# Rows of score maxima written by VectorE, an earlier place for the first expert slot's tokens, and two DMAs for the norm's gains

## The chip, the cores and the metric

One NeuronCore of one Trainium2 chip runs the whole program. The metric is the device time of one execution in microseconds (us), and smaller is better. The engines are named as in the profile: PE (matrix multiplications and transposes), DVE (VectorE), ACT (ScalarE), POOL (GpSimd) and SP (which issues most DMAs).

## The reference

Attention with normalized queries and keys feeds a mixture of experts in which each token goes to one expert:

```python
def _attn_ref(q, k, v, g_q, g_k):          # q, k, v: (8, 12, 448, 64)
    def rmsnorm(x, g):
        return x / np.sqrt(np.mean(x * x, axis=-1, keepdims=True) + 1e-06) * g
    q_n, k_n = (rmsnorm(q, g_q), rmsnorm(k, g_k))
    scores = np.matmul(q_n, k_n.transpose(0, 1, 3, 2)) / np.sqrt(64)
    scores = scores - np.max(scores, axis=-1, keepdims=True)
    attn = np.exp(scores)
    attn = attn / (np.sum(attn, axis=-1, keepdims=True) + 1e-09)
    return np.matmul(attn, v)

def _moe_ref(x, modality_id, w_gate, modality_bias, w1, w2):   # x: (3584, 768), 8 experts, F = 1024
    logits = x @ w_gate + modality_bias[modality_id]
    e_idx = np.argmax(logits, axis=1)
    probs = softmax(logits)
    for e in range(8):
        mask = e_idx == e
        h = np.maximum(x[mask] @ w1[e], 0.0)
        out[mask] = probs[mask, e][:, None] * (h @ w2[e])
```

All arrays are float32. The kernel keeps that precision by splitting operands into a rounded high part and a rest, and summing the products of parts.

## The kernel before, in words

**Attention** runs over 48 units; a unit is two heads of one batch entry. One loop walks steps n from -22 to 335, seven steps to a unit; each step j of unit u issues one block of 128 score rows. For each unit, `load` brings q and k, `sumsq` (line 836) squares them on ACT and sums the squares on DVE, `rstd` and `norm` (line 886) scale them, `tr` (line 900) transposes them on PE and splits them into parts, with the product of the two gain vectors, `gs`, multiplied into k. The four DMAs of `load_gains` (line 127) fetch the gains, `gain_product` (line 133) multiplies them.

Scores are computed twice. First `sa` (line 979) makes the high parts' product in blocks of 128 rows, and DVE takes each block's negated maxima into a column of `mx` (128 x 7; `at_hlw` in the rows). `mt` (line 998) transposes `mx` on PE to 7 x 128; ACT copies that from PSUM to `ms`, and a DMA lays the seven rows end to end as one row, number 64 of the tile `ql`. It is issued from ACT's queue for units 0, 1 and 45 to 47, else from SP's. Then `st` (line 1011) makes the scores transposed, with full parts: a matmul with 128 rows, and a second with 65, in which row 64 of the keys' tile `kh` is all ones, so that the row of maxima is subtracted. ACT takes the exponential, `av` (lines 1051 to 1060) multiplies with the values, and `avcopy` (line 1067) copies the result out of PSUM, on ACT for most units. `sa` and `tr` have two PSUM buffers each, `st` two, `av` one. In the first units PE also runs filler matmuls (`warm`, line 1341), whose number at each step is in the table `PLAN`.

**The experts** run on 14 static slots of 256 tokens and a tail. Of the first slot the tokens are brought in while attention ends: `xgather` (line 550) gathers them on POOL's queue, `xkeep` (line 555) stores them to DRAM, `xfetch` (line 559) fetches them back in four pieces, both on SP's queue, and `xturn` (line 574) transposes a third of them on DVE; ACT then casts the third to its high part in `xw`, and DVE takes the rest. `split1` (line 531) splits the first weights in the same way. The first expert matmul is `ph` (line 608).

**The order of the work** is written out, not found by the hardware: `PLAN` (line 34) gives the step at which each piece is due, and the loop (lines 1424 to 1544) hands pieces to lists that are emptied at a step: `pre["A"]` on ACT and `pre["V"]` on DVE ahead of the step's exponential, `post` behind it. Each engine executes its own list strictly in that order and waits on semaphores.

In the rows, `w1w`, `xw`, `r2w`, `xrw`, `at_hlw` and similar are large tiles that several buffers share; line L52 is a helper through which DVE, ACT and POOL instructions are recorded. `w1w` holds `ql`, and `w1w<-xw 7x128` is thus the row of maxima.

## Time and profile before

| | us |
|---|---|
| median of three runs | 1041.73 |
| lowest and highest | 1040.16, 1044.53 |
| profiled execution | 1043.32 |
| its span in the trace | 1041.5 |
| PE busy | 1017.7 (98%) |
| DVE, ACT, POOL busy | 742.2 (71%), 710.0 (68%), 718.2 (69%) |

The profile is one execution; what lies outside the span (1.8 us) is start and end. Attention takes the first 541 us or so, the experts the rest. [...]

### The profile page before, as it was taken

To read this page: it belongs to the slowest core of one execution; us is meant where nothing else is said; L and a number is where in the kernel's file an instruction comes from. 1 tells how busy PE (TensorE), PEld (TensorE's weight loads), DVE (VectorE), ACT (ScalarE), POOL (GpSimd) and SP (SyncE) were. 2 spreads that over 40 slices of the span, in tenths; PEclk is the share of its full clock that TensorE was granted. 3 is DMA by queue.
4 is the path that set the end of the run, shared out by engine and by line. 5 is a ranking of instruction groups with operands and counts; after the bars stand their busy time and mean duration, and the time that the engine had idled before them with its cause. 6 is when DMAs were issued, how large, how long until landed. Compare 5 with 4: busy or idle time off the path is not lost.

```text
span 1041.5 us, 18863 instructions
## 1 busy us (share of the span) xinstructions
PE 1017.7 (98%) x6462; PEld 820.2 (79%) x6462; DVE 742.2 (71%) x1260; ACT 710.0 (68%) x1379; POOL 718.2 (69%) x747
## 2 busy tenths in 40 slices
PE   8999999999999999999999999999999999999996
PEld 7655666666666666656659999999999999999995
DVE  5777888887888778886667987755675567656740
ACT  6897999889999889887655555645554455545531
POOL 6788798989788887888956646765645555565451
PEclk9999999999999999999999999999999999999998
DMA  6775658868677677665748506234572343234261
GB/s 181 193 172 131 160 139 191 166 143 183 157 170 160 156 177 156 163 119 119 230 120 285 92 17 188 71 92 122 162 263 74 110 122 92 62 92 123 74 201 63
DMA packets 147960, 148.20 MB, mean 142 GB/s; under 512 B 72762, under 2 KB 137742, under 8 KB 147344
## 3 DMA queue, kind: packets, MB, share of 16 engines
q1 hardware_dynamic: 122458, 105.08, 42.7%
q0 software_dynamic: 25328, 41.82, 12.8%
q8 instruction: 53, 0.87, 0.4%
q14 instruction: 51, 0.42, 0.2%
q10 hardware_dynamic: 70, 0.02, 0.0%
HBM read 150.31 MB, written 33.39 MB: 176 GB/s over the span
## 4 chain that ended last, share of the span: by engine, by line
PE 85%; DMA 4%; DVE 3%; ACT 3%; issue 2%; POOL 1%; SPq 1%; ACTq 0%; POOLq 0%; DVEq 0%
PE ph L608 23%; PE py L638 22%; PE st L1018 12%; PE av L1060 10%; PE sa L990 5%; PE av L1056 3%; PE tr L908 3%; PE xt L1126 2%; PE sm L1082 2%; DVE at_hlw L52 1%; PE sm L1089 1%; DMA w1w<-xw 1%; PE mt L1001 1%; DMA xrw<-xg 1%; DMA r<-in_q_dram 1%
## 5 line engine op out<-in xcount | busy, mean ns | idle before, releaser
L608 PE MATMUL ph<-xw,w1w 128*128 128x256 f32 x2016 | 246.3, 283 | 2.1 <-ACT at_w2lw L52 1.3
L608 PEld LDWEIGHTS ph<-xw,w1w 128*128 128x128 f32 x2016 | 243.9, 192 | 3.9 <-ACT at_w2lw L52 1.4
L52 DVE TENSOR_REDUCE at_hlw<-sa 128x1 f32<-128x448 f32 x336 | 205.0, 619 | 30.3 <-PE sa L985 15.2
L1018 PE MATMUL st<-w1w 128*128 128x448 f32 (+1 forms) x480 | 183.4, 431 | 1.5 <-ACT r2w L52 0.9
L52 POOL DMA_INDIRECT r<-in_moe_w_dram,tb_w x60 | 84.6, 1411 | 54.9 <-DVE w1w L52 39.7
L52 ACT ACTIVATE hhw<-ph 128x512 fp32r<-128x512 f32 x56 | 33.5, 598 | 123.4 <-PE ph L608 94.3
L52 ACT ACTIVATE r2w<-st 128x448 f32<-128x448 f32 x168 | 91.1, 545 | 34.6 <-PE st L1018 23.2
L638 PE MATMUL py<-w2lw,hhw 128*128 128x384 f32 x448 | 113.7, 334 | 0.0
L52 DVE TENSOR_TENSOR w1w<-r,w1w 128x768 fp32r<-128x768 f32 x112 | 104.9, 968 | 11.0 <-ACT w1w L52 9.8
L990 PE MATMUL sa<-w1w 128*128 128x448 f32 (+1 forms) x288 | 108.1, 376 | 3.0 <-DVE at_hlw L52 1.2
L52 ACT CAST w1w<-xw 64x448 fp32r<-64x448 f32 x188 | 105.9, 563 | 3.7 <-issue 1.4
L52 POOL DMA_INDIRECT r2w<-in_moe_w_dram,tb_vi x48 | 51.5, 1074 | 81.7 <-DVE w2lw L52 68.1
L52 DVE TENSOR_TENSOR w2lw<-r2w,w2ha 128x1536 fp32r<-128x1536 f32 x28 | 49.1, 1757 | 80.0 <-ACT w2ha L52 49.2
L1018 PEld LDWEIGHTS st<-w1w 128*128 128x128 f32 (+1 forms) x480 | 86.0, 190 | 24.6 <-issue 10.9
L1018 PE MATMUL st<-w1w,w2ha 65*128 65x448 f32 x288 | 100.6, 370 | 0.5 <-DMA w1w<-xw 0.5
L52 ACT ACTIVATE at_w2lw<-st 128x448 f32<-128x448 f32 x168 | 90.6, 545 | 12.5 <-PE st L1018 5.7
L52 POOL TENSOR_TENSOR xrw<-r,at_hlw 112x512 f32<-112x512 f32 x95 | 97.8, 1050 | 0.5
L52 POOL TENSOR_TENSOR r2w<-r2w 128x448 f32<-128x448 f32 (+1 forms) x72 | 83.3, 1157 | 21.3 <-DVE r2w L52 15.0
L52 ACT CAST w1w<-r 128x768 fp32r<-128x768 f32 x112 | 95.2, 903 | 0.1
L52 ACT ACTIVATE yw<-py,ltn 128x384 f32<-128x384 f32 x55 | 29.4, 579 | 77.0 <-PE py L638 48.5
L638 PEld LDWEIGHTS py<-w2lw,hhw 128*128 128x128 f32 x448 | 80.9, 188 | 0.0
L52 POOL TENSOR_TENSOR r2w<-r2w,at_w2lw 64x448 f32<-64x448 f32 (+1 forms) x48 | 55.3, 1151 | 32.8 <-DVE r2w L52 17.4
(302 smaller groups left out, 2210.2 us busy)
## 6 DMA issues: line engine op xcount, KB each, us to landing
w1w<-xw SPq DMA_DIRECT2D x216, 112.0 KB
xg<-xrw SPq DMA_DIRECT2D x14, 768.0 KB
xrw<-xg SPq DMA_DIRECT2D x56, 192.0 KB
r<-in_q_dram SPq DMA_DIRECT2D x19, 448.0 KB
r<-in_k_dram SPq DMA_DIRECT2D x19, 448.0 KB
w2ha<-xw SPq DMA_DIRECT2D x72, 112.0 KB
w1w<-w1w SPq DMA_DIRECT2D x48, 112.0 KB
r2w<-in_v_dram SPq DMA_DIRECT2D x24, 224.0 KB
```

Of the source, the lines that this page charges most:

```text
L52: return fn(*a, **kw)
L608: PE.matmul(ps[:, i], lhsT=lt_, rhs=rt_[:, c], start=n == 0, stop=n == 17)
L638: PE.matmul(ps[n][:, :384], lhsT=lt_[:, j, 128 * t : 128 * t + 128], rhs=rt_[:, 384 * n : 384 * n + 384], start=j == 0 and m == 0, stop=j ...
L908: PE.transpose(sp[:, c], src[:, c], idn[:CP, :CP])
L990: PE.matmul(ps[:, :S], lhsT=t["qq"][r, h, a : a + 128], rhs=t["kk"][h][r], start=True, stop=True)
L1001: PE.transpose(ps[0:NJ, :128], t["mx"], idn)
L1018: PE.matmul(ps[:, :S], lhsT=l, rhs=t["qq"][:, h] if first else t["ql"][0:65, h], start=first and (j != 3 or h == 0), stop=not first and (j ...
L1056: PE.matmul(t["av"][:, :S], lhsT=vd_b[u % 2], rhs=t["p"][:, 3], start=False, stop=True)
L1060: PE.matmul(t["av"][64 * h : 64 * h + 64, :S], lhsT=vv[:, u % 3, j], rhs=t["p"][:, j], start=c == 0, stop=False)
L1082: PE.matmul(R[g][32 * i : 32 * i + 32, :S], lhsT=sel[:, m], rhs=T[u + i // 2]["cs"][:, i % 2], start=m == 0, stop=False, tile_position=(0, ...
L1089: PE.matmul(sm[32 * i : 32 * i + 32, :S], lhsT=wg[:, (4 * g + i) % NP], rhs=T[4 * g + i]["xt"], start=False, stop=True, tile_position=(0, ...
L1126: PE.transpose(ps[:CP, 128 * c : 128 * c + 128], T[u]["xt"][:, c * CP : (c + 1) * CP], idn)
```

## The change

**Rows of maxima.** For units 0, 1, 45, 46 and 47 (`by_rows`) `mx` is the last seven columns of a tile of 71 whose first 64 are zero. `mt` transposes all 71, so that the maxima land on partitions 64 to 70 of PSUM. One DVE multiplication of 7 x 896 then writes rows 64 to 70 of `ql`: the seven rows, repeated seven times along the row, times a block of the identity, so that row 64 + j holds the maxima of block j at their place and zeros elsewhere. The keys' tiles get seven rows of ones, and the second score matmul of these units has 71 rows. ACT's copy and the DMA of these units go.

**Gains.** `load_gains` issues two DMAs, each of which reads a gain vector twice and writes 128 partitions. `gain_product` is called ahead of the norm of queries of unit 0 instead of behind the norm of its keys.

**First slot.** `xkeep` moves from step 317 to 315, `xfetch` from 320 to 317, and the three `xturn` from steps 330, 332, 334 to 327, 329, 331. `split1` in unit 47 moves from its steps 1 and 4 to 4 and 6.

**Fillers.** The `warm` entries of steps -7, -6 and -5 go (three, one and one).

```diff
-'warm': {-22: 15, -21: 3, -20: 1, -16: 4, -15: 1, -13: 5, -10: 2, -7: 3, -6: 1, -5: 1, 5: 1, 7: 1}
+'warm': {-22: 15, -21: 3, -20: 1, -16: 4, -15: 1, -13: 5, -10: 2, 5: 1, 7: 1}
...
-'s1': (1, 4)
+'s1': ((1, 4), (4, 6))
...
-            for half in range(2):
-                SY.dma_start(gg[64 * half : 64 * half + 64, 0:1], g_q.unsqueeze(1))
-                SY.dma_start(gg[64 * half : 64 * half + 64, 1:2], g_k.unsqueeze(1))
+            for i, g in enumerate((g_q, g_k)):
+                SY.dma_start(gg[:, i : i + 1], bass.AP(tensor=g.tensor, offset=g.offset, ap=[[0, 2], [1, 64], [1, 1]]))
...
+    KR = 64 + NJ
+    kh_f = [view(w2ha, WZ * i, KR, WZ) for i in range(3)] + [view(w1w, 4 * ST, KR, WZ)]
...
+    mw_b = [view(sw, SS + 288 + 72 * i, 128, KR) for i in range(2)]
+    mx_b = [m[:, 64:KR] for m in mw_b]
+
+    def by_rows(u):
+        return u < 2 or u >= NU - 3
...
+            G.memset(kh[64:KR].bitcast(F32), 1.0)
...
+        for m in mw_b:
+            G.memset(m[:, 0:64], 0.0)
...
+            if by_rows(u):
+                PE.transpose(ps[0:KR, :128], mw_b[u % 2], idn)
+                sh = [NJ, NJ, 128]
+
+                def rows():
+                    V.tensor_tensor(
+                        out=t["ql"][64:KR].rearrange("p h s -> p (h s)").rearrange("p (j c) -> p j c", j=NJ),
+                        in0=ps[64:KR, :128].unsqueeze(1).to_broadcast(sh),
+                        in1=idn[64:KR, 64:KR].unsqueeze(2).to_broadcast(sh), op=ALU.mult)
+
+                return rows
...
+                    kr = 128 if first else KR if by_rows(u) else 65
+                    PE.matmul(ps[:, :S], lhsT=l[:kr], rhs=t["qq" if first else "ql"][:kr, h],
...
-        LD0, XRJ = 0, (1, 3, 5)
+        LD0, XRN = 0, (327, 329, 331)
...
-                at(pre["A"], n + 1, mt(*a))
+                at(pre["V" if by_rows(*a) else "A"], n + 1, mt(*a))
...
+                if a == (0, 0):
+                    gain_product()
                 norm(*a, V if a in P["nv"] else G)
-                if a == (0, 1):
-                    gain_product()
...
-            if n == NJ * (NU - 3) + 2:
+            if n == 315:
                 xkeep(0)
-            if n == NJ * (NU - 3) + 5:
+            if n == 317:
                 xfetch(0)
-            if i >= NU - 2 and j in P["s1"]:
-                split1(P["s1"].index(j), i - NU + 2)
+            if i >= NU - 2 and j in P["s1"][i - NU + 2]:
+                split1(P["s1"][i - NU + 2].index(j), i - NU + 2)
```

Three pieces of the engines' lists show how instructions move. On DVE, in the first norms (`at_hlw<-xrw` is a sum of squares, `xrw<-r_0` the norm of unit 0's queries), before:

```order
L52 TENSOR_REDUCE at_hlw<-xrw 112x8 x2
L52 TENSOR_TENSOR gs<-gg 128x1
L52 TENSOR_SCALAR gs<-gs 128x1
L52 TENSOR_REDUCE at_hlw<-xrw 112x8 x2
L52 MEMSET w2ha 65x3x64
L52 MEMSET w1w 65x64
L52 TENSOR_TENSOR xrw<-r_0_158,at_hlw 112x2x4x64
```

The same place after the change:

```order
L52 TENSOR_REDUCE at_hlw<-xrw 112x8 x4
L52 TENSOR_TENSOR gs<-gg 128x1
L52 TENSOR_SCALAR gs<-gs 128x1
L52 MEMSET w2ha 71x3x64
L52 MEMSET w1w 71x64
L52 TENSOR_TENSOR xrw<-r_0_158,at_hlw 112x2x4x64
```

The gains' product stands behind four sums of squares instead of between two and two.

On DVE around the maxima of unit 0 (`at_hlw<-sa` are maxima of unit 1, `mt` the transposed maxima of unit 0), before:

```order
L52 TENSOR_REDUCE at_hlw<-xrw 112x8
L52 SCALAR_TENSOR_TENSOR xw<-tr_1_386,gs,xw 128x448
L52 TENSOR_REDUCE at_hlw<-sa_0_423 128x1
L52 TENSOR_REDUCE at_hlw<-sa_1_430 128x1
L52 TENSOR_REDUCE at_hlw<-sa_2_434 128x1
```

The same place after the change:

```order
L52 TENSOR_REDUCE at_hlw<-xrw 112x8
L52 SCALAR_TENSOR_TENSOR xw<-tr_1_386,gs,xw 128x448
L52 TENSOR_TENSOR w1w<-mt_391,idn 7x896
L52 TENSOR_REDUCE at_hlw<-sa_0_417 128x1
L52 TENSOR_REDUCE at_hlw<-sa_1_424 128x1
L52 TENSOR_REDUCE at_hlw<-sa_2_428 128x1
```

A multiplication of 7 x 896 stands ahead of the maxima of unit 1.

On ACT at the passage from attention to the experts (`xw<-r2w` casts a third of the tokens, `xrw<-av45` copies the result of unit 45, `st47` are exponentials of unit 47, `w1w<-r1_1` is a weight split), before:

```order
L52 ACTIVATE r2w_163<-st46_5_6296 128x448
L52 ACTIVATE r2w_163<-st46_6_6306 128x448
L52 COPY xrw_160<-av45_6241 128x448
L52 ACTIVATE lo6_6248<-lo6_6248 112x32
L52 ACTIVATE at_w2lw_167<-st47_0_6314 128x448
L52 ACTIVATE at_w2lw_167<-st47_1_6325 128x448
L52 CAST w1w_161<-r1_1_159 128x768
L52 ACTIVATE at_w2lw_167<-st47_2_6337 128x448
L52 CAST xw_162<-r2w_163 128x512
```

The same place after the change:

```order
L52 ACTIVATE r2w_163<-st46_5_6286 128x448
L52 ACTIVATE r2w_163<-st46_6_6297 128x448
L52 CAST xw_162<-r2w_163 128x512
L52 COPY xrw_160<-av45_6232 128x448
L52 ACTIVATE lo6_6239<-lo6_6239 112x32
L52 ACTIVATE at_w2lw_167<-st47_0_6307 128x448
L52 ACTIVATE at_w2lw_167<-st47_1_6319 128x448
L52 CAST xw_162<-r2w_163 128x512
L52 ACTIVATE at_w2lw_167<-st47_2_6330 128x448
```

The cast of the first third stands ahead of the copy of av45, where it stood behind three exponentials of unit 47 and a weight split; that split stands later. On SP no row changes its place.

## Rows read from the trace of the kernel before

**Rows 1.** The page, part 1: busy us, share of span, instructions.
```profile
PE 1017.7 (98%) x6462; PEld 820.2 (79%) x6462; DVE 742.2 (71%) x1260; ACT 710.0 (68%) x1379; POOL 718.2 (69%) x747
```

**Rows 2.** Busy time by stretches: PE, PEld, DVE, ACT, POOL, granted clock, DMA, GB/s.
```profile
core 0: us, PE busy (x) PEld busy (x) DVE busy (x) ACT busy (x) POOL busy (x), PEclk, DMA share, GB/s
11.90:15.30 3.40, 3.27 (x16) 3.28 (x16) 1.35 (x3) 3.34 (x9) 2.36 (x7) 0.51 0.48 147
100.00:490.00 390.00, 387.66 (x2124) 243.76 (x2124) 319.69 (x637) 345.46 (x802) 328.40 (x369) 1.00 0.71 157
528.00:538.00 10.00, 8.56 (x44) 4.96 (x43) 7.67 (x10) 7.33 (x17) 6.06 (x6) 1.00 0.31 88
```

**Rows 3.** Timeline, all engines, 5 to 13 us: start, us, engine, line, operation.
```profile
6.97 0.32 SPq L833 DMA_DIRECT2D r<-in_q_dram  x1
7.55 1.15 ACT L52 ACTIVATE xrw<-r 112x512 f32<-112x512 f32 x2 [0.83 <-DMA r<-in_k_dram]
...
9.10 0.60 PE L908 MATMUL tr<-idn,xrw 112*128 112x112 f32 x4 [0.27 <-POOL xrw L52]
...
9.61 0.16 DVE L52 TENSOR_TENSOR gs<-gg 128x1 f32<-128x1 f32 x1 [3.57 <-DMA gg<-in_g_k_dram]
...
9.88 1.27 DVE L52 TENSOR_REDUCE at_hlw<-xrw 112x8 f32<-112x512 f32 x2
11.35 0.62 DVE L52 TENSOR_TENSOR xrw<-r,at_hlw 112x512 f32<-112x512 f32 x1
...
12.03 1.01 PE L908 MATMUL tr<-idn,xrw 112*128 112x112 f32 x4 [2.08 <-DVE xrw L52]
```

**Rows 4.** Timeline, PE, ACT and DVE around the maxima of unit 0.
```profile
25.20 1.73 PE L1341 MATMUL warm<-idn,ones 128*128 128x128 f32 x14
26.05 0.24 ACT L52 CAST xw<-mt 7x128 fp32r<-7x128 f32 x1
...
26.32 1.32 ACTq L52 DMA_DIRECT2D w1w<-xw  x1
...
27.17 1.81 DVE L52 TENSOR_REDUCE at_hlw<-sa 128x1 f32<-128x448 f32 x3 [0.31 <-PE sa L990]
...
27.68 0.56 ACT L52 CAST w1w<-xw 64x448 fp32r<-64x448 f32 x1 [1.39 <-issue]
...
30.48 0.44 PE L1018 MATMUL st<-w1w,w2ha 65*128 65x448 f32 x1 [0.49 <-DMA w1w<-xw]
```

**Rows 5.** The page, part 5: two groups of 128x768, mean ns of one.
```profile
L52 DVE TENSOR_TENSOR w1w<-r,w1w 128x768 fp32r<-128x768 f32 x112 | 104.9, 968 | 11.0 <-ACT w1w L52 9.8
...
L52 ACT CAST w1w<-r 128x768 fp32r<-128x768 f32 x112 | 95.2, 903 | 0.1
```

**Rows 6.** Waits of SP's queue, 495 to 545 us: in total, times, longest.
```profile
SPq L556 <- DMA xrw<-x_d,ltn: 7.4, 1, 7.4
...
SPq L562 <- DMA xg<-xrw: 5.0, 1, 5.0
```

**Rows 7.** Timeline, PE, ACT and DVE at the passage to the experts.
```profile
527.71 0.53 ACT L52 COPY xrw<-av 128x448 f32<-128x448 f32 x1 [0.15 <-PE av L1056]
...
528.42 1.72 PE L1060 MATMUL av<-r2w,at_w2lw 128*64 128x448 f32 x8
...
530.65 1.19 DVE L52 STREAM_TRANSPOSE r2w<-xrw 128x512 f32<-128x512 f32 x1 [1.82 <-DMA xrw<-xg]
...
531.88 0.62 ACT L52 CAST xw<-r2w 128x512 fp32r<-128x512 f32 x1 [0.47 <-DVE r2w L52]
...
537.56 1.70 PE L608 MATMUL ph<-xw,w1w 128*128 128x256 f32 x12 [1.25 <-ACT at_w2lw L52]
...
539.81 0.38 PE L608 MATMUL ph<-xw,w1w 128*128 128x256 f32 x1 [0.54 <-ACT xw L52]
...
540.53 0.85 PE L608 MATMUL ph<-xw,w1w 128*128 128x256 f32 x5 [0.35 <-DVE xw L52]
...
541.32 0.97 PE L1060 MATMUL av<-at_w2lw 128*64 128x448 f32 x4
```

**Rows 8.** The page, part 3: main DMA queue, packets, MB, share of 16 engines.
```profile
q1 hardware_dynamic: 122458, 105.08, 42.7%
```

More of the change, by code (lines that the diff above doesn't have):

```diff
@@ L453 @@
     kk_f = [view(w1w, ST * i + W, 128, WZ) for i in range(4)]
-    kh_f = [view(w2ha, WZ * i, 65, WZ) for i in range(3)] + [view(w1w, 4 * ST, 65, WZ)]
+    KR = 64 + NJ
+    kh_f = [view(w2ha, WZ * i, KR, WZ) for i in range(3)] + [view(w1w, 4 * ST, KR, WZ)]
     zeros = [view(t, o, p, n, d)[:, :, S : S + 64] for t, o, p, n, d in (
-        (w1w, W, 128, 4, ST), (w2ha, 0, 65, 3, WZ), (w1w, 4 * ST, 65, 1, WZ))]
+        (w1w, W, 128, 4, ST), (w2ha, 0, KR, 3, WZ), (w1w, 4 * ST, KR, 1, WZ))]
     def two(t):
@@ L484 @@
     ra_b, rz_b = SS + 48 * 4, SS + 48 * 5
-    mx_b = [view(sw, SS + 288 + 8 * i, 128, NJ) for i in range(2)]
+    mw_b = [view(sw, SS + 288 + 72 * i, 128, KR) for i in range(2)]
+    mx_b = [m[:, 64:KR] for m in mw_b]
+    def by_rows(u):
+        return u < 2 or u >= NU - 3
     rs_b = [cp.tile([CP, NCH, 4, 2], F32, name=f"rs{i}") for i in range(2)]
@@ L1017, in st @@
                 for h, l in columns(t["kkf" if first else "khf"], j):
-                    PE.matmul(ps[:, :S], lhsT=l, rhs=t["qq"][:, h] if first else t["ql"][0:65, h],
+                    kr = 128 if first else KR if by_rows(u) else 65
+                    PE.matmul(ps[:, :S], lhsT=l[:kr], rhs=t["qq" if first else "ql"][:kr, h],
                               start=first and (j != 3 or h == 0), stop=not first and (j != 3 or h == 1))
@@ L1471 @@
                 puts.pop(0)[1]()
-            if i == NU - 1 and j in XRJ:
-                at(post, n + 1, xturn(0, XRJ.index(j)))
+            if n in XRN:
+                at(post, n + 1, xturn(0, XRN.index(n)))
             run(pre["A"], n)
```

6 lines of the change are left out of this document (2 added, 4 removed).

## Prediction

> **What bounds the kernel now.** I read the busy times of the page first: PE works 98% of the span [rows 1]. The table by stretches confirms it for the long middle: of 390 us in the attention units PE is idle 2.3, while DVE has 70 and ACT 45 to spare [rows 2]. So a saving on DVE or ACT in the middle is worth nothing, and the change can only matter where PE stands still. Two places do, and I read both in the timeline: the first 31 us, where the units fill the pipeline, and the passage from attention to the experts at 528 to 541 us. At the start the reader should see one instruction on DVE, the product of gains `gs`, that idles 3.57 us for its DMA with two reductions queued behind it, and PE, which then stands 2.08 us for the norm that needs them [rows 3]. [...] At the passage PE idles 1.25, 0.54 and 0.35 us ahead of the first expert matmuls [rows 7].
>
> An edge of 0.5%, about 5.2 us, is what a measurement of this kernel can tell from no change. Sums are made against the profiled execution (1043.3 us, 1.6 above the median of 1041.7); I apply the differences to the median.
>
> **Gains product, behind four reductions instead of two.** The squares that feed the second pair are done at 8.70 (7.55 + 1.15) [rows 3]. The second pair takes 1.27, so without `gs` ahead it ends near 9.35, inside the time DVE idles now. `gs` comes when its data comes, and its two steps end at 9.96. The norm starts 0.20 after DVE is free (11.15 to 11.35), so at 10.16 instead of 11.35: **1.2 us sooner**. The two DMA issues that fall away save SP some 1.2, but its next load goes out at 6.97, after a wait that began before the issues would matter [rows 3]; I count nothing, and lose at most as much if the new form is slow (third rival).
>
> **Clock at the start.** PE's idle time shrinks from 2.08 to about 0.9. After 1.25 us of idle at 537 the granted clock stayed at 1.00 [rows 2, 7], so I take the fall away. Its price is at most 1.7, half of the 3.4 us at low clock; the same four transposes took 1.01 there and 0.60 before [rows 3]. ACT is nearly as busy in that stretch as PE (3.34 against 3.27 of 3.40), so part of the time would pass anyway: bounds 0 and 1.7, **0.9 taken**, the middle.
>
> **Rows of maxima on DVE, five units.** For unit 0 the change removes ACT's copy (0.24), the DMA issue after which ACT stood 1.39, and the DMA for which PE waited 0.49 at the second score matmul; ten warm matmuls of some 0.12 go too (14 took 1.73) [rows 4]. It adds a DVE multiplication of 7x896 ahead of three reductions. No row shows that shape: 128x768 takes 968 ns [rows 5], so 1.1 by length, between 0.97 and 1.3 if reading PSUM through a repeated view costs a little. The reductions are thus later by about 1.1, against 1.2 less on PE before their matmuls; PE's wait of 0.49 goes. **0.5 gained**, with ends of −0.6 (the row is on the path, 1.1 less 0.49) and 1.1 (the row hides). For units 1 and 45 to 47 the rows lie in DVE's idle 18%, and ACT's relief is worth nothing since PE sets the pace [rows 2]. If that cover were gone, each would cost 1.1. K of 71 instead of 65 changes no column count.
>
> Start in sum: 1.2 + 0.9 + 0.5 = **2.6 us sooner**, ends 0.6 and 4.0. It moves everything behind it alike, as PE is what the units wait for.
>
> **Tokens of the first slot.** The storing and fetching DMAs get earlier step numbers, but SP's own list is the same before and after, row by row. SP already waits 7.4 us for the gather to land and 5.0 us for the store to land [rows 6]; the gather's place on POOL does not move. So the tokens land when they do now, and the first transpose on DVE starts at 530.65, after 1.82 of waiting [rows 7]. I count **nothing gained**.
>
> **What is placed behind them.** The transposes do move: the first now stands ahead of a DVE multiplication, and ACT's cast of its result stands ahead of the copy of av45, where it stood behind three exponentials before. ACT therefore waits for the tokens: the cast runs at 531.88 for 0.62 as now, the copy of av45 (0.53, now at 527.71) ends near 533.0. The next value matmuls need the one PSUM buffer which that copy frees; they start at 528.42 now and at 533.0 then, 4.6 later [rows 7]. From there to the value matmuls at 541.32 it is 12.9 us now, of which 2.1 are the three idle times; the rest is PE work, 10.8, and the remaining transposes and casts fit beside it, since tokens are there by then. So those matmuls start at 543.8 instead of 541.3: **2.5 lost** with a full clock. The store of a finished block on SP is 4.6 later also; SP issues nothing else up to 545, so I give it no price. The weight splits that move later lie in the new slack of DVE and ACT; the last of them on ACT (0.9 [rows 5]) stands ahead of the exponential that frees the buffer of the first expert matmul, and it ends about when PE arrives.
>
> The clock is the open price. PE would stand 4.6 us, more than twice the 2.08 after which it was seen at the low level. By that nearest row I take a fall again, costing 1.7 (half of 3.4). Ends: 0 and 1.7 and, if low clock lasts longer, 3.4. **Passage in sum: 4.2 lost**, ends 2.5 and 5.9.
>
> Sum: −2.6 + 4.2 = +1.6; the profiled execution would take 1044.9, the median **1043.3 us**, no change by the edge above.
>
> **Rivals.**
> *First: PE's clock holds through the stall* (activity before it is unlike that at the start, where filler matmuls ran). Then −2.6 + 2.5 = −0.1, 1041.6 us. For it: the clock held through 1.25 idle. Against: the fall after 2.08.
>
> *Second: the tokens do come sooner,* as the edit of the step numbers says. Then the casts find them and the 2.1 idle at the passage goes too: −2.6 − 2.1, 1037.0 us. Against: SP's list is unchanged and its waits are for landings. For: less traffic from ACT's queue and an earlier gather could shorten two waits that make up 12.4 us.
>
> *Third, slower: the gains come later.* Now four DMAs write 64 partitions each; then two write 128, their source led by a dimension of two copies. If each is carried by only two engines, one engine moves 64 packets where it moved few. The mean packet of the main queue takes 58 ns (42.7% of 16 engines' span over 122458 packets [rows 8]), so 3.7 us at most, and for four bytes probably less. Then `gs` is done at 13.7, the norm 2.5 later than now rather than 1.2 sooner, and the fall of clock stays. The start is 2.0 late (2.5 less 0.5), with the passage +6.2: 1047.9 us. It decides from about 2.7 us of delay, 42 ns per packet.
>
> [...] No row here shows how many engines carried the gains.
>
> **How the numbers follow.** The forecast has 0.50, the first rival 0.22, the second 0.12, the third 0.08; 0.08 is left for what I do not see. The forecast's own range is 1041.9 to 1045.3 (start 4.0 or 0.6, passage 4.2). The range to give is 1038.5 to 1046.5: it holds forecast and first rival, the half of the second in which only some idle time goes, and stops short of the third. Faster by over 0.5% (under 1036.5) needs the second rival with the start at its upper end: 0.05. Slower (over 1046.9) is the third and a passage at its upper end: 0.09. The rest, 0.86, is no change.
>
> **What would show it.** Right, if `gs` comes after four reductions with the norm near 10.2, no clock below 1.00 from 11 to 16, the second score matmul of unit 0 near 28 without a DMA wait, ACT idle for some 3 us ahead of the cast at the passage, and PE idle 4 to 5 us ahead of av46 with a low clock behind it. Wrong, if the first transpose starts well before 527.9 (530.65 less the start's 2.6 would be no gain), if PE's idle time at the passage shrinks, or if `gs` starts after 10.

## The result, and the profile after

| | before | after |
|---|---|---|
| median of six runs each, us | 1040.95 | 1052.43 |
| lowest and highest, us | 1039.63, 1044.53 | 1047.19, 1054.75 |
| profiled execution, us (its span) | 1043.32 (1041.5) | 1050.57 (1048.8) |

The ratio is 1.0095 (95%: 1.0073 to 1.0117): slower by about 1%. The prediction was no change, 1043.3 us (1.6 slower) with a range up to 1046.5, so it was wrong: 11.5 slower was measured. The profiled executions differ by 7.3 us, less than the medians (11.5): before's lies 2.4 above its median, after's 1.9 below. The traces account for the 7.3.

To find where the time went I took one event that each of the 48 units has, the start of its transposed maxima (`mt`), and subtracted before from after. The numbers are worked out from the two traces, in us:

```
mt of unit     0     2    19    20    21    32    33    34    44    47   first ph   last ph
           -3.2  -3.0  -3.0  +3.1  +3.0  +2.7  +4.7  +3.3  +2.2  +2.0   +7.3       +7.3
```

There are three steps. The start is 3.0 sooner, and that holds up to unit 19. Between unit 19 and unit 20, 6.1 us are lost at one stroke. From unit 47 to the first expert matmul (`ph`) another 5.3 go. The small steps between (−0.4, +2.0, −1.4, −1.1, −0.2) come to −1.1. Start and passage were predicted (−2.6 and +4.2); the middle was not.

The page of after, part 1 and one group of part 5 (line, engine, operation; busy, mean ns | idle before, releaser), and then the same group in before:

```profile
PE 1017.0 (97%) x6452; PEld 819.9 (78%) x6452; DVE 747.1 (71%) x1265; ACT 708.8 (68%) x1374; POOL 706.9 (67%) x749
...
L997 PE MATMUL sa<-w1w 128*128 128x448 f32 (+1 forms) x288 | 108.4, 377 | 9.9 <-DMA w1w<-xw 6.8
```

```profile
L990 PE MATMUL sa<-w1w 128*128 128x448 f32 (+1 forms) x288 | 108.1, 376 | 3.0 <-DVE at_hlw L52 1.2
```

Against [rows 1], PE has ten instructions less and 0.7 us less work; DVE has 4.9 us more, which the rows bring, but it is not the engine that the units wait for. What grew is PE's idle time, and the group shows where. Ahead of these score matmuls PE stood idle 3.0 us in all before and 9.9 after, 6.8 of them for a DMA that moves keys or queries from `xw` to `w1w`.

**The start.** Timeline of after, 8 to 28 us (start, us, engine, line, operation, [idle before <- releaser]):

```profile
7.78 1.28 DVE L52 TENSOR_REDUCE at_hlw<-xrw 112x8 f32<-112x512 f32 x2 [1.99 <-ACT xrw L52]
...
9.11 0.16 DVE L52 TENSOR_TENSOR gs<-gg 128x1 f32<-128x1 f32 x1
...
9.66 0.62 DVE L52 TENSOR_TENSOR xrw<-r,at_hlw 112x512 f32<-112x512 f32 x1
...
10.33 0.60 PE L915 MATMUL tr<-idn,xrw 112*128 112x112 f32 x4 [0.24 <-DVE xrw L52]
...
23.68 1.09 DVE L52 TENSOR_TENSOR w1w<-mt,idn 7x896 fp32r<-7x896 f32 x1
...
27.47 0.37 PE L1036 MATMUL st<-w1w,w2ha 71*128 71x448 f32 x1
```

`gs` starts right behind the reductions (7.78 + 1.28 = 9.06) and shows no wait for a DMA; the norm is at 9.66 instead of 11.35 and PE's transposition at 10.33 instead of 12.03 [rows 3]. The new multiplication takes 1.09 us, and the second score matmul runs at 27.47 without a wait, where it ran at 30.48 [rows 4].

**The middle and the passage.** Busy time of after by stretches (us, PE, PEld, DVE, ACT, POOL, PE's granted clock as a share of the full one, DMA share, GB/s):

```profile
11.00:15.00 4.00, 4.00 (x28) 3.18 (x26) 2.71 (x5) 3.92 (x11) 2.23 (x9) 1.00 1.02 231
228.50:232.70 4.20, 0.00 (x0) 0.00 (x0) 0.67 (x2) 1.29 (x3) 3.74 (x4) 1.00 1.09 172
232.70:237.00 4.30, 4.25 (x16) 1.96 (x16) 2.43 (x4) 2.19 (x4) 2.78 (x4) 0.60 0.56 123
528.40:534.80 6.40, 1.71 (x7) 0.92 (x5) 2.42 (x4) 1.60 (x4) 0.00 (x0) 0.93 0.43 96
534.80:538.50 3.70, 3.65 (x9) 1.24 (x10) 3.41 (x5) 1.61 (x4) 1.29 (x2) 0.50 0.60 186
```

At the start the clock stays at 1.00, where before had 0.51 [rows 2]. In unit 19 PE does nothing at all for 4.2 us, and the next 4.3 us run at a mean of 0.60: that is the step of 6.1. At the passage PE stands, and then runs at 0.50.

Which waits these are, first on PE at 218 to 240 us of after:

```profile
PE sa L997 <- DMA w1w<-xw: 4.3, 1, 4.3
```

Before has no wait of PE in that stretch. In this unit SP issues four such moves of keys and queries one behind the other (line 928 of after, 921 of before). The semaphore that PE waits for tells which of them it is: the last but one, issued at 224.83. Timeline of after, SP, POOL and PE between the transposed maxima of unit 19 (220.34) and unit 20 (237.39):

```profile
222.38 2.35 SPq L928 DMA_DIRECT2D w1w<-xw  x1
...
224.83 1.70 SPq L928 DMA_DIRECT2D w1w<-xw  x1
...
225.55 0.97 POOL L1251 DMA_INDIRECT l_d<-ltk,posi  x1 [0.16 <-issue]
...
226.58 0.59 SPq L928 DMA_DIRECT2D w1w<-xw  x1
...
232.75 0.44 PE L997 MATMUL sa<-w1w 128*128 128x448 f32 x1 [4.28 <-DMA w1w<-xw]
```

The same place in before, where unit 19's transposed maxima are at 223.35:

```profile
226.69 1.96 SPq L921 DMA_DIRECT2D w1w<-xw  x1
...
228.57 0.98 POOL L1233 DMA_INDIRECT l_d<-ltk,posi  x1 [0.16 <-issue]
...
228.70 0.59 SPq L921 DMA_DIRECT2D w1w<-xw  x1
```

The last move's issue on SP takes 0.59 in both. In after the two issues ahead of it are held (2.35 and 1.70), in before one is (1.96). So the issue of the last but one ends 6.18 us after the unit's transposed maxima instead of 5.29, and the last move goes out right behind it, at 6.23 instead of 5.35. The scatter of routing results `l_d` on POOL is issued at the same point of the unit in both (its issue ends at 6.18 and 6.20). In after PE gets the data 7.9 us after the issue of the last but one began (232.75 − 224.83); in before PE never waits.

The trace has the landings of these DMAs as updates of their semaphores, up to 16 for each. In after PE starts 0.14 us behind the last update for the move that it waits for (232.61 and 232.75), so the last one is taken as the landing. From them one can work out who came when, in us from unit 19's transposed maxima (`after_again` is a second trace of after, without the stall; see below):

```
              last but one: issue    landed    scatter landed    last move landed
before             3.33 to 5.29       6.94          11.68              7.63
after_again        4.58 to 5.99       7.71          12.66             12.83
after              4.48 to 6.18      12.27          12.10             12.44
```

The scatter is slow in all three. In before and `after_again` the move that PE needs is through ahead of it. In after the ten last parts of that move come each 0.16 to 0.18 us behind a part of the scatter: the move lands behind the scatter, and PE stands until then.

The held issues go with loads of the engines' own instructions, which have DMA queues of their own. Part 3 of after's page (queue: packets, MB, share):

```profile
q8 instruction: 53, 0.87, 0.4%
q14 instruction: 51, 0.42, 0.2%
```

These are 53 loads of 16 KB and 51 of 8 KB, each kind some 20 us apart on the average. In before the 8 KB load of that unit is over 0.4 us after its transposed maxima and the 16 KB load lasts from 2.5 to 5.0; in after the 8 KB load lasts from 2.0 to 4.3 and the 16 KB load from 3.9 to 5.8. The two held issues of after lie beside these two loads. That is so throughout: of the moves from `xw` to `w1w` issued between 100 and 500 us in the twenty traces of this document, 118 have an issue of over 1.2 us, and 117 of these overlap a load. But 735 others overlap one too and are not held, and where an issue is held the load is long as well (2.3 us for 8 KB here, where the middle one of that trace takes 0.4). So load and issue are held together; which holds which no run shows. Nothing that the change edits stands in that unit. What differs is how many instructions each engine had run by then, and where the loads fall (2.0 and 3.9 instead of 0.1 and 2.5); that the second comes from the first is my reading, which the experiments test.

### The profile page after: what moved, and what is told of

Its sections match the earlier page's. It is cut to its first block, busy times and chain, and to the rows that moved or that the text cites. A ratio compares the mean times of both kernels' runs of the same rounds, so it can differ in the third digit from the quotient of the medians.

```text
span 1048.8 us, 18838 instructions
## 1 busy us (share of the span) xinstructions
PE 1017.0 (97%) x6452; PEld 819.9 (78%) x6452; DVE 747.1 (71%) x1265; ACT 708.8 (68%) x1374; POOL 706.9 (67%) x749
## 4 chain that ended last, share of the span: by engine, by line
PE 83%; DVE 4%; DMA 4%; issue 4%; POOL 2%; ACT 2%; SPq 1%; POOLq 0%; DVEq 0%; ACTq 0%
PE ph L613 20%; PE py L643 19%; PE st L1036 13%; PE av L1078 11%; PE sa L997 5%; PE tr L915 3%; PE av L1074 3%; PE xt L1144 2%; DMA w1w<-xw 2%; PE sm L1100 2%; DMA xrw<-xg 1%; DVE at_hlw L52 1%; PE sm L1107 1%; PE sa L992 1%; PE mt L1019 1%
## 5 line engine op out<-in xcount | busy, mean ns | idle before, releaser
L1036 PE MATMUL st<-w1w 128*128 128x448 f32 (+2 forms) x480 | 184.4, 434 | 0.9 <-ACT r2w L52 0.7
L52 POOL DMA_INDIRECT r<-in_moe_w_dram,tb_w x60 | 79.2, 1321 | 56.9 <-DVE w1w L52 41.6
L52 POOL DMA_INDIRECT r2w<-in_moe_w_dram,tb_vi x48 | 48.5, 1010 | 90.7 <-DVE w2lw L52 82.3
L1036 PEld LDWEIGHTS st<-w1w 128*128 128x128 f32 (+2 forms) x480 | 86.8, 192 | 23.8 <-issue 11.1
L1036 PE MATMUL st<-w1w,w2ha 65*128 65x448 f32 (+1 forms) x288 | 100.4, 369 | 0.0
```

Source lines behind the costliest of these rows:

```text
L52: return fn(*a, **kw)
L1036: PE.matmul(ps[:, :S], lhsT=l[:kr], rhs=t["qq" if first else "ql"][:kr, h], start=first and (j != 3 or h == 0), stop=not first and (j != 3 ...
```

## The experiments

Each kernel was timed beside runs of the kernel before on the same chip; the ratio is against those. "Rows" are the maxima written by DVE, "fillers" the ten matmuls taken away with the `warm` entries of steps −7 to −5 (five in all, two matmuls each). The text that stands behind each edit says what was expected before the run.

| kernel | median, us (lowest to highest, runs) | ratio (95%) |
|---|---|---|
| tok_only | 1047.53 (1044.02 to 1050.76, 10) | 1.0050 (1.0034 to 1.0065) |
| no_tok | 1050.00 (1048.60 to 1051.40, 4) | 1.0077 (1.0060 to 1.0094) |
| gains_only | 1039.47 (1038.66 to 1046.29, 10) | 0.9975 (0.9956 to 0.9995) |
| rows_only | 1052.43 (1048.11 to 1056.08, 4) | 1.0108 (1.0078 to 1.0138) |
| rows45 | 1041.39 (1040.02 to 1043.80, 10) | 0.9982 (0.9966 to 0.9999) |
| warm_only | 1046.15 (1043.26 to 1051.46, 10) | 1.0032 (1.0011 to 1.0053) |
| rows_warm | 1043.56 (1039.88 to 1050.82, 10) | 1.0007 (0.9977 to 1.0036) |
| tok_split | 1047.98 (1044.39 to 1051.70, 8) | 1.0047 (1.0024 to 1.0070) |
| rows_pad | 1041.86 (1040.68 to 1047.75, 10) | 1.0000 (0.9981 to 1.0020) |
| xturn_only | 1046.30 (1044.00 to 1048.37, 10) | 1.0041 (1.0023 to 1.0058) |
| gains_rows45 | 1038.80 (1037.32 to 1041.10, 10) | 0.9960 (0.9945 to 0.9975) |
| no_tok_warm | 1041.58 (1037.73 to 1044.72, 10) | 0.9979 (0.9958 to 1.0000) |
| after_warm | 1043.22 (1041.19 to 1050.32, 10) | 1.0023 (1.0003 to 1.0043) |
| after_again | 1052.11 (1042.74 to 1053.79, 9) | 1.0099 (1.0083 to 1.0116) |
| rows_again | 1051.72 (1048.22 to 1052.18, 3) | 1.0083 (1.0058 to 1.0109) |
| tok_split_again | 1041.49 (1037.26 to 1046.69, 8) | 0.9994 (0.9971 to 1.0016) |
| after_put | 1051.35 (1045.71 to 1055.62, 10) | 1.0066 (1.0034 to 1.0097) |
| gr_put | 1040.15 (1038.54 to 1044.08, 10) | 0.9969 (0.9943 to 0.9996) |

**The parts alone.** The first four kernels split the change: the tokens, all but the tokens, the gains, and the rows with the fillers gone.

`tok_only`, before with the tokens' part:

```diff
-        LD0, XRJ = 0, (1, 3, 5)
+        LD0, XRN = 0, (327, 329, 331)
...
-            if n == NJ * (NU - 3) + 2:
+            if n == 315:
...
-            if n == NJ * (NU - 3) + 5:
+            if n == 317:
...
-'s1': (1, 4)
+'s1': ((1, 4), (4, 6))
```

> The kernel before with the first slot's tokens alone as in the change: store, fetch, transposes and weight splits at the new steps; rows by DMA and four gain DMAs as before. Theory P (the passage): ACT's first cast stands ahead of the copy of av45 and waits for the tokens; the first expert matmul comes about 5 us later than in the kernel before (542 to 543 us instead of 537.6) with nothing changed ahead of 520 us: slower by 4 to 6 us. Rival J (a DMA landing late in the middle, at unit 20, is the main loss, and the passage is paid back): at most 1 us slower. Rival of my prediction (tokens land sooner): faster by 2.

In its trace the distance to before goes from +1.7 at unit 47 to +6.5 at the first expert matmul: the passage loses 4.8, where the change loses 5.3. Two more losses are in this trace: 2.1 us in unit 20, to which we come back, and 1.1 in the experts (+7.6 at the end).

`no_tok`, the change with the tokens' part undone:

```diff
-        LD0, XRN = 0, (327, 329, 331)
+        LD0, XRJ = 0, (1, 3, 5)
...
-            if n == 315:
+            if n == NJ * (NU - 3) + 2:
...
-            if n == 317:
+            if n == NJ * (NU - 3) + 5:
...
-'s1': ((1, 4), (4, 6))
+'s1': (1, 4)
```

> The changed kernel with the tokens' steps and the weight splits as before; rows on DVE, two gain DMAs and the shorter warm list stay. Theory P: the passage is again as in the kernel before, 5 us faster than the changed kernel (1045 to 1048 if the late landing at unit 20 stays, 1037 to 1039 if it does not, as the start gains 3). Rival J: the late landing at unit 20 stays and costs 6, so the time is about 1044 to 1046 and the gain of the start is gone.

It stays slow: at unit 19 it is 2.7 ahead, at unit 20 it is 4.6 behind, a stroke of 7.3 us at the place where the change loses 6.1. From unit 47 to the first expert matmul it then loses 0.3 only (and 2.0 later, in the experts). Middle and passage are thus two separate losses.

`gains_only`, before with the gains' part:

```diff
-            for half in range(2):
-                SY.dma_start(gg[64 * half : 64 * half + 64, 0:1], g_q.unsqueeze(1))
-                SY.dma_start(gg[64 * half : 64 * half + 64, 1:2], g_k.unsqueeze(1))
+            for i, g in enumerate((g_q, g_k)):
+                SY.dma_start(gg[:, i : i + 1], bass.AP(tensor=g.tensor, offset=g.offset, ap=[[0, 2], [1, 64], [1, 1]]))
...
+                if a == (0, 0):
+                    gain_product()
                 norm(*a, V if a in P["nv"] else G)
-                if a == (0, 1):
-                    gain_product()
```

> The kernel before with two gain DMAs and the gains' product ahead of the norm of queries, nothing else. Gain of the start from the gains alone: norm of unit 0's queries at 9.7 instead of 11.35, no low clock from 11.9 to 15.3: the transposed maxima of unit 0 come 1.7 to 3 us sooner, 1038 to 1039.5. If the late landing at unit 20 comes with any earlier start, it is slower than before by 3; then row landings at unit 20 lag behind the scatter of the routing as in the changed kernel.

The units run 2.6 to 3.1 sooner from unit 2 to unit 33 (3.0 in the change up to unit 19), and 4.4 to 4.6 from there, since unit 33 lasts 10.5 us instead of 11.9: a wait of 0.94 that PE has there in before, for the last but one of the moves, is gone. The median gains 0.25%.

`rows_only`, before with the rows of all five units, as in the change, and without the fillers (of the edits for the rows only `by_rows` is shown, here and below):

```diff
-'warm': {-22: 15, -21: 3, -20: 1, -16: 4, -15: 1, -13: 5, -10: 2, -7: 3, -6: 1, -5: 1, 5: 1, 7: 1}
+'warm': {-22: 15, -21: 3, -20: 1, -16: 4, -15: 1, -13: 5, -10: 2, 5: 1, 7: 1}
...
+    def by_rows(u):
+        return u < 2 or u >= NU - 3
```

> The kernel before with rows of maxima written by DVE for five units and the shorter warm list, nothing else. By the sum of the prediction 0.5 faster, between 1.1 faster and 0.6 slower: 1039.9 to 1041.6. If the rows are what brings the late landing at unit 20, it stands in this trace too and the time is 1045 to 1048.

In the median it is as slow as the whole change. Its trace is of the quickest of its four executions (1048.11), 4.8 us over before's, and it loses 6.5 by one wait of PE at 358 to 380 us, far from any row that it edits:

```profile
PE sa L998 <- DMA w1w<-xw: 3.9, 1, 3.9
```

Unit 32 lasts 16.1 us instead of 9.6. So the stroke is not tied to unit 19; it comes with this part of the change. What the slower executions lose beyond that no trace shows.

**Which of the two, rows or fillers?** `rows45`, rows for the last three units alone, fillers kept:

```diff
+    def by_rows(u):
+        return u >= NU - 3
```

> Rows by DVE for units 45 to 47 alone; units 0 and 1 by DMA, the warm list of before. Lists on ACT, DVE, PE and SP are those of before up to unit 45, so theory C has the middle unchanged: 1040 to 1043, and the difference at the last three units is within 1 us. If rows by DVE cost where they stand, the transposed maxima of units 45 to 47 and the first expert matmul come 1 to 4 us late.

`warm_only`, before without these `warm` entries, nothing else:

```diff
-'warm': {-22: 15, -21: 3, -20: 1, -16: 4, -15: 1, -13: 5, -10: 2, -7: 3, -6: 1, -5: 1, 5: 1, 7: 1}
+'warm': {-22: 15, -21: 3, -20: 1, -16: 4, -15: 1, -13: 5, -10: 2, 5: 1, 7: 1}
```

> The kernel before without the five filler matmuls of steps -7 to -5, nothing else (their ten matmuls and ten weight loads on PE go). Theory C (where the instruction loads fall): PE's 16 KB loads come about 1.6 us later relative to the work; at unit 20 the load then meets SP's issues of the moves elsewhere. If the fillers' removal is the cause of the rows kernel's late landings, a stall of 4 to 7 us stands at unit 20 or 33 and the time is 1045 to 1051. If it is ACT's shorter list, this kernel takes 1040 to 1042. Theory of the work itself: 0 to 1.2 us faster.

`rows_warm`, the rows of all five units with the fillers kept:

```diff
+    def by_rows(u):
+        return u < 2 or u >= NU - 3
```

> Rows of maxima by DVE for five units with the warm list of before kept, so that PE's list has its old length (one matmul more). Theory C with PE's list as the cause: no late landing beyond those of before, 1040 to 1042. With ACT's list as the cause (six instructions shorter by unit 20, DVE's three longer): late landings at unit 20 or 33 as in rows alone, 1046 to 1052.

The last three units' rows are harmless: from unit 44 to the first expert matmul the trace of `rows45` gains 0.6 us. Ten fillers fewer at the very start cost 0.3% of the median and in the trace 4.2 us in unit 32 (13.8 instead of 9.6). The rows with fillers kept cost nothing that the interval shows, but four of their ten executions took 1046.2 to 1050.8, and the trace, of one of these, loses 2.2 in unit 33.

**Length or place?** `rows_pad` takes the same five fillers away but adds five at step −20, the very start, so that PE's list keeps its length:

```diff
-'warm': {-22: 15, -21: 3, -20: 1, -16: 4, -15: 1, -13: 5, -10: 2, -7: 3, -6: 1, -5: 1, 5: 1, 7: 1}
+'warm': {-22: 15, -21: 3, -20: 6, -16: 4, -15: 1, -13: 5, -10: 2, 5: 1, 7: 1}
...
+    def by_rows(u):
+        return u < 2 or u >= NU - 3
```

> Rows by DVE for five units without the fillers of steps -7 to -5 (as the run of rows alone), but with five more fillers at step -20, in the time in which PE waits for the first norm; PE's list has again the length of before from unit 0 on. Theory C (the place of PE's instruction loads): no late landing beyond those of rows with the warm list kept, 1041 to 1045. If the fillers matter by their own work where they stood (between the maxima of unit 0 and the scores of unit 1), the loss of rows alone stays: 1048 to 1056.

It is as fast as before, 1.0000, against 1.0108 of `rows_only`, which has the same work at the same steps but for fillers in the first microseconds. At unit 2 the two traces are level (0.4 and 0.6 ahead of before). Its waits of PE at 358 to 380 us:

```profile
PE sa L998 <- DMA w1w<-xw: 0.8, 1, 0.8
```

So the cost is not that PE lacks fillers where they stood. It goes with the number of instructions ahead of everything else.

`after_warm` does the same to the whole change, with the entries kept:

```diff
-'warm': {-22: 15, -21: 3, -20: 1, -16: 4, -15: 1, -13: 5, -10: 2, 5: 1, 7: 1}
+'warm': {-22: 15, -21: 3, -20: 1, -16: 4, -15: 1, -13: 5, -10: 2, -7: 3, -6: 1, -5: 1, 5: 1, 7: 1}
```

> The changed kernel with the five fillers of steps -7 to -5 kept, all else as in the change. Theory C with P: no stall of over 4 us at units 20 or 33, the start's 3 us kept, the passage 4.4 late as with the transposes alone: 1043 to 1046, 7 to 9 under the changed kernel. If the fillers matter only where rows come without the gains and the tokens: 1050 to 1054.

`no_tok_warm` keeps them too, and undoes the tokens' part as `no_tok` does:

```diff
-'warm': {-22: 15, -21: 3, -20: 1, -16: 4, -15: 1, -13: 5, -10: 2, 5: 1, 7: 1}
+'warm': {-22: 15, -21: 3, -20: 1, -16: 4, -15: 1, -13: 5, -10: 2, -7: 3, -6: 1, -5: 1, 5: 1, 7: 1}
...
-        LD0, XRN = 0, (327, 329, 331)
+        LD0, XRJ = 0, (1, 3, 5)
```

> Gains and rows for five units with the warm list and the tokens' steps of before: the changed kernel less its tokens part and less the removal of the fillers. Theory C: the start's 3 us stay to the end, 1039 to 1042, with no stall of over 4 us at unit 20. If rows alone bring the late landings in the middle, 1046 to 1050, as with the fillers removed.

With the tokens' part, ten fillers are worth 8.9 us in one series on one chip (1052.11, `after_again` below, to 1043.22); without it the ratio goes from 1.0077 to 0.9979. Neither trace has the stall. That of `no_tok_warm` loses 4.6 us inside the experts, for which I have no cause.

**How steady is it?** `after_again` is the changed kernel unchanged, `rows_again` and `tok_split_again` repeat those two:

> The changed kernel once more, for a second trace. Theory C: the stall of 6 us stands at unit 20 or 33 again, with two SP issues of over 1.3 us in a row (or one of over 3) ahead of it, each beside a load of instructions. If the stall of the first trace was chance, there is none, and the time is 1043 to 1046.

> Rows by DVE without the fillers once more, for a second trace. Theory C: a stall of over 4 us at unit 20 or 33 again. If chance: none, 1041 to 1043.

Eight of nine executions of `after_again` took 1050.04 to 1053.79, one 1042.74, and that one was profiled. So one kernel has both outcomes, and its trace shows what is missing in the quick one. Busy time of `after_again`, 225 to 242 us:

```profile
225.00:242.00 17.00, 17.00 (x94) 10.97 (x87) 13.97 (x23) 15.57 (x37) 15.07 (x19) 1.00 0.88 166
```

PE works all the time at full clock. The last move of unit 19 went out at 6.04 there, 0.19 sooner than in the execution with the stall, and ahead of the end of the scatter's issue (6.18); so did the last but one, which PE needs first. `rows_again` in turn has the stall in unit 19 (18.1 us instead of 10.9), where `rows_only`, the same kernel, had it in unit 32. Its busy time by stretches:

```profile
230.00:234.50 4.50, 0.32 (x1) 0.35 (x2) 0.48 (x1) 1.11 (x3) 4.22 (x5) 0.80 1.00 172
234.50:239.00 4.50, 4.50 (x14) 2.27 (x15) 2.43 (x4) 2.19 (x4) 2.23 (x4) 0.50 0.45 100
```

Again an idle stretch, and then 0.50. The table sets the traces side by side for unit 19. Loads are given by start and duration, all in us from the unit's transposed maxima. "Last move" is when it was issued, which is right behind the issue of the last but one; the scatter's issue ends at 6.16 to 6.20 except in `after_put` (7.36):

```
kernel        rows  fillers   8 KB load    16 KB load   last move   unit lasts
before        no    kept      0.1 (0.3)    2.5 (2.5)    5.35        10.9
rows45        some  kept      0.1 (0.5)    2.5 (3.0)    5.91        10.9
warm_only     no    gone      0.1 (0.5)    4.0 (2.0)    3.85        10.9
rows_warm     yes   kept      1.8 (2.6)    2.5 (2.9)    5.63        10.9
rows_pad      yes   moved     1.8 (2.9)    2.5 (2.6)    5.49        10.9
after_warm    yes   kept      1.8 (2.8)    2.5 (3.1)    5.99        10.9
rows_only     yes   gone      1.8 (2.3)    3.8 (1.5)    5.59        10.9
after_again   yes   gone      1.8 (2.5)    3.8 (1.8)    6.04        10.9
after         yes   gone      2.0 (2.3)    3.9 (1.9)    6.23        17.0
rows_again    yes   gone      1.8 (2.5)    3.8 (2.1)    6.27        18.1
no_tok        yes   gone      1.8 (2.7)    3.8 (2.1)    6.30        18.3
after_put     yes   gone      1.7 (0.6)    4.1 (2.5)    3.85        10.9
```

The rows of the first units, which shorten ACT's list, go with a shift of the 8 KB load by 1.7 us. The missing fillers, which shorten PE's list by ten matmuls and ten weight loads, go with a shift of the 16 KB load by 1.3 to 1.5; at the 181 instructions in 17 us of the row of `after_again` above, twenty take 1.9. One trace breaks the rule: `tok_only` keeps the fillers, and its lists are those of before up to unit 44, yet its 16 KB load starts at 4.0. It is the trace that loses 2.1 in unit 20. So a load can fall late by itself; without the fillers it did in all seven traces, with them in one of thirteen. From these shifts I take a load to be due at a place in an engine's list and not at a time; that is an estimate, and `tok_only` speaks against it. With the rows alone the two loads overlap, with the missing fillers alone the 8 KB load is long past; with both, one follows the other and SP's issues are held twice. In unit 32 the same pattern holds: the last move goes out at 4.5 of 9.6 us in before, at 5.62 in `rows_only` and at 6.36 in `warm_only`, behind the end of the scatter's issue (5.61 there), and these are the units that take 16.1 and 13.8.

**Is it the order against the scatter?** In every trace but the next, units 19 and 32 lose over 1.8 us if, and only if, the last move is issued behind the scatter. The landings say the same of the move that PE needs: the nine longest waits of PE for a move in the twenty traces (1.3 to 4.4 us, from 60 to 525 us) all end on a move that lands 0.17 to 0.51 us behind a scatter, at once or with other moves in between. `after_put` tests it by putting the scatters one step later:

```diff
-            if puts and n >= puts[0][0] and n - lastput[0] >= 3:
+            if puts and n > puts[0][0] and n - lastput[0] >= 3:
```

> The changed kernel with the routing's scatters one step later on POOL (behind one more operation of 1.1 us), all else as in the change. Theory S, read from 18 traces: the stall stands at unit 20 or 32 exactly where the last move is issued after the issue of the scatter has ended. With the scatter 1.1 later, moves issued 6.0 to 6.3 us behind the maxima of unit 19 come ahead of its end, so no stall of over 4 us at unit 20: 1043 to 1046, as with the fillers kept. If the order against the scatter is not the cause (code loads or other traffic hold the moves themselves), the stall stays: 1050 to 1054.

It missed: 1051.35, no quicker than the change. Unit 19 lasts 10.9 as it should, but the loads changed their durations too, and unit 20 lost 4.2 in turn. There the needed move is behind the next scatter, issued just ahead of that unit: a last part of this scatter lands at 8.57 us of unit 20, and three moves follow 0.17 apart, the needed one at 9.08. `tok_only` loses its 2.1 in unit 20 in the same way. PE's waits at 215 to 250 us:

```profile
PE sa L997 <- DMA w1w<-xw: 1.3, 1, 1.3
PE st L1036 <- DMA w1w<-xw: 0.9, 1, 0.9
```

The place of the needed move behind a scatter is thus seen in every one of these stalls, but no edit here has taken it away and brought the time back. What the runs show is the condition and its price: with the fillers gone from PE's list alone 0.3%, with ACT's list shorter too 0.8 to 1.1%.

**The passage.** `xturn_only` moves the three transpositions alone, to test the prediction's step by itself:

```diff
-        LD0, XRJ = 0, (1, 3, 5)
+        LD0, XRN = 0, (327, 329, 331)
...
-            if i == NU - 1 and j in XRJ:
-                at(post, n + 1, xturn(0, XRJ.index(j)))
+            if n in XRN:
+                at(post, n + 1, xturn(0, XRN.index(n)))
```

> The kernel before with the three transposes alone at their new steps; weight splits, store and fetch as before. Theory P: ACT's cast ahead of the copy of av45 stands for the tokens, PE stands 4 to 5 us ahead of av46 with a low clock behind it, the expert matmuls come 4 to 6 us late: 1045 to 1049. If the later weight splits are needed for the loss, under 2 us.

From −0.7 at unit 47 to +3.7 at the end: 4.4 us, where 4.2 had been predicted for the passage (at the first expert matmul it is +5.4, of which some is won back behind it). Its timeline at the passage:

```profile
530.81 1.07 DVE L52 STREAM_TRANSPOSE r2w<-xrw 128x512 f32<-128x512 f32 x1 [4.30 <-DMA xrw<-xg]
531.91 0.62 ACT L52 CAST xw<-r2w 128x512 fp32r<-128x512 f32 x1 [5.05 <-DVE r2w L52]
532.44 0.53 ACT L52 COPY xrw<-av 128x448 f32<-128x448 f32 x1
...
533.02 3.25 PE L1060 MATMUL av<-r2w,at_w2lw 128*64 128x448 f32 x8 [3.84 <-ACT xrw L52]
```

DVE, ACT and PE wait one behind the other for tokens that land when they did before (530.65 [rows 7]), and the eight value matmuls take 3.25 us instead of 1.72.

`tok_split` is the counterpart: store, fetch and weight splits moved as in `tok_only`, the transpositions at their old steps (330, 332, 334):

> The kernel before with the store and fetch numbers and the later weight splits of the change, but the three transposes at their old steps. Theory P (transposes ahead of the copy make the stall): the passage is as before, first expert matmul within 0.5 us, 1040 to 1043. If the later weight splits or the fetch make the loss, the first expert matmul is late here too by 4 to 6 us: 1046 to 1049.

> Later weight splits with the transposes at their old steps once more, for a second trace. In the first one PE stood 0.81 us and then 2.51 us at 552 to 556 us with a low clock behind it, as its load of instructions started 2.9 us later than in the kernel before, beside the first slot's weights. If that is what makes this kernel slow, it stands there again, and the time is 1045 to 1050; else the loss lies elsewhere in this trace.

The first series gave 1.0047. But its passage lost nothing, and its time went later, at 552 to 556 us. The repeat of the same kernel gave 0.9994, with no loss anywhere. I draw from it only that early fetches without early transpositions gain nothing, and that two series of one kernel, on two chips, can lie 6.5 us apart.

**The parts that gain.** `gains_rows45` joins the gains with the rows of the last three units, and leaves out the rest:

```diff
+            for i, g in enumerate((g_q, g_k)):
+                SY.dma_start(gg[:, i : i + 1], bass.AP(tensor=g.tensor, offset=g.offset, ap=[[0, 2], [1, 64], [1, 1]]))
...
+    def by_rows(u):
+        return u >= NU - 3
```

> Two gain DMAs and the earlier gains product, and rows by DVE for units 45 to 47 alone; warm list, tokens and splits of before. If both parts add up: 3 from the start and 1 from the last units, 1038 to 1039. Theory C: the middle may take 2 to 6 us more or less in single executions, as lists are two shorter on SP, but the median stays under the kernel before.

It beats both kernels: 1038.80, 0.4% under before, with the upper end at 0.9975. `gr_put` adds the later scatters to it:

```diff
-            if puts and n >= puts[0][0] and n - lastput[0] >= 3:
+            if puts and n > puts[0][0] and n - lastput[0] >= 3:
```

> Gains, rows of maxima for units 45 to 47, and the scatters one step later: a version meant to keep the best parts clear of the stall. Theory S: 1037 to 1040, no unit in the middle over 12.2 us, and a spread below that of the kernel before. If the later scatter meets other moves or delays POOL's own work, 1040 to 1046.

Nothing more is gained (1040.15, 0.9969).

## Why the prediction was wrong, and where it was right

**Gains and clock at the start: right.** Predicted 2.6 sooner with the rows' share, measured 3.0, and 2.8 by the gains alone, where 2.1 (1.2 + 0.9) had been summed for them. The rows' own 0.5 can't be told apart: traces whose start is untouched lie at unit 2 up to 1.6 us ahead of before (`tok_split`), and that of `rows45`, which only adds memsets there, 1.8 behind it. What was said to show it is there: `gs` behind four reductions, no clock below 1.00 from 11 to 15 (the row above), the second score matmul near 28 (27.47) without a DMA wait. The norm came at 9.66 instead of the 10.16 I had worked out, since `gs` did not wait for its data, which I had taken to come when it came before.

**The third rival, later gains: false.** `gs` starts 0.50 sooner than before (9.11 against 9.61). What the trace shows of how these DMAs are carried is their semaphores' updates: each of the two DMAs of after makes one soon after its issue (4.85 and 5.47) and only two more (the last at 7.71 and 9.01), where each of the four of before makes sixteen (the last at 9.54). That two engines carried each, which was the rival's condition, no run shows; the updates tell only that the new form lands in three steps instead of sixteen. Its price in this place was none: the data was there 0.05 us ahead of the end of the reductions. That it was there at all by then is luck; I had it come no sooner than before.

**Rows on DVE: the work was right, the count was not.** The multiplication takes 1.09 (I said 1.1), the second score matmul takes 369 ns with 71 rows as with 65 (means of after), and PE's DMA wait is gone. I booked "ten warm matmuls of some 0.12 go too" as a saving of PE time, and ACT's copies and issues as relief that is worth nothing. That is the step that failed, together with "It moves everything behind it alike, as PE is what the units wait for". Both treat a removed instruction as work only, and the loss in the middle got no term at all. What the runs showed in its place: with the fillers gone, loads of instructions fall later (the 16 KB load of unit 19 at 3.9 us instead of 2.5), beside SP's issues, and 200 us on a move that PE needs lands behind a scatter (12.27 and 12.10), PE is idle for 4.3 us and its clock at 0.50 for 3.4, 6.1 us in the trace. In the median the fillers are worth 8.9 us (`after_again` against `after_warm`). The outcome lay in the 0.09 for slower, but not by the third rival or the passage, for which I gave it. With the rest of the change as it is, `after_warm` has a median of 1043.22, 1.4 over its own before, where 1.6 had been the sum. That this fits so well is in part luck: its trace, of the quickest execution, is 1.8 ahead of before at the last expert matmul, by 2.0 us won in the middle and 2.6 won behind the first expert matmul, which no term of the sum names.

**Tokens land no sooner: right.** SP's two waits are 6.7 and 6.2 against 7.4 and 5.0 [rows 6], 12.9 us against 12.4:

```profile
SPq L561 <- DMA xrw<-x_d,ltn: 6.7, 1, 6.7
SPq L567 <- DMA xg<-xrw: 6.2, 1, 6.2
```

The first transposition starts at 532.64, 2.0 later than before, as all units there are. The second rival is false.

**What stands behind them: right.** Timeline of after at the passage:

```profile
532.64 1.07 DVE L52 STREAM_TRANSPOSE r2w<-xrw 128x512 f32<-128x512 f32 x1 [3.87 <-DMA xrw<-xg]
533.74 0.62 ACT L52 CAST xw<-r2w 128x512 fp32r<-128x512 f32 x1 [4.57 <-DVE r2w L52]
534.27 0.53 ACT L52 COPY xrw<-av 128x448 f32<-128x448 f32 x1
...
534.85 3.25 PE L1078 MATMUL av<-r2w,at_w2lw 128*64 128x448 f32 x8 [4.74 <-ACT xrw L52]
```

The cast holds the copy, the copy holds the buffer, and PE stands 4.74 us (4.6 predicted) and then runs at 0.50 from 534.8 to 538.5, so the first rival, a clock that holds, is false. ACT stands 4.57 ahead of the cast, where some 3 had been said. The low level cost 1.5 on those eight matmuls (3.25 less 1.72), where I took 1.7. The sum was made at the value matmuls that start at 541.32 before [rows 7]; they start at 547.23 after. Counted from unit 47's transposed maxima that is 4.0 lost, and in the same way 4.6 in `xturn_only` and 3.4 in `tok_only`: 4.2 had been predicted, with ends of 2.5 and 5.9. At the first expert matmul, which comes ahead of them, it is 5.3.

**What stays open.** Why the last parts of unit 19's scatter land 6.9 us after its issue began, and 6.5 in before; whether the loads hold SP's issues or both are held by a third thing; why the stall falls now on unit 19, now on unit 32, and in one execution of nine on neither; why `tok_only` has a late load with all its fillers; and the losses inside the experts of `no_tok_warm` and of the first `tok_split`. That the 8 KB load of unit 19 is ACT's and the 16 KB load PE's is inferred from which edit shifts which load; the 51 loads of q14 are too many for ACT's 1374 instructions if q8 has 53 for PE's 12904 (matmuls and weight loads), so q14 seems to serve other engines as well. A kernel in which a load alone is shifted, with no instruction of the units changed but at other steps, was not tried beyond `rows_pad`.

## What to carry to other kernels

An edit that adds or removes instructions early in a program can also move later instruction loads (here by 1.3 to 1.7 us, 200 us on); where a late DMA issue can stop the bound engine (here for 4.3 us), test the edit a second time with the list's length restored by harmless instructions, before you judge the edit itself. An instruction that waits for a late DMA must not be put ahead of one that frees a buffer: moving the consumer earlier does not bring the data (here PE stood 4.74 us). And time the parts of a change apart: here two parts that gain were hidden under two that lose.

## What the runs showed of the hardware that was not expected

- Some issues of a DMA on SP that take 0.59 us otherwise take 2.35 and 1.70 us beside an instruction load (222.38 and 224.83 of after); of 118 moves with an issue of over 1.2 us, 117 overlap a load.
- A move whose issue ends with that of a scatter on POOL, or after it, can land behind the scatter: 12.27 against 12.10 us of unit 19 in after, where it landed at 6.94 in before.
- A delay of 0.2 us in one issue (its end at 5.99 or 6.18, the scatter's at 6.18) goes with 6.1 us more for the unit (17.0 instead of 10.9): PE's idle time of 4.3 is followed by 3.4 us at a clock of 0.50 (233.6 to 237.0 of after).
- Ten filler matmuls in the first 27 us decide over 8.9 us in the median (1052.11 and 1043.22); in the traces the stalls come 200 to 350 us later.
- Medians of eight runs of one kernel on two chips lay 6.5 us apart (1047.98 and 1041.49).
